# FNet and product-key experts in one kernel: scales summed by the matrix engine, second keys earlier, row sums spread over four blocks

## The chip, the cores and the metric

One core of a Trainium2 chip runs the whole program. The metric is its device time in microseconds (us). The engines are PE (TensorE, matmuls), DVE (VectorE), ACT (ScalarE), POOL (GpSimd) and SP (SyncE, which here only issues DMAs). Each engine works through its own list in order; an instruction waits for semaphores of other engines, and everything behind it on its engine waits with it. The programming layer places each instruction into its engine's list by a scheduler, so the order in a list isn't the order of the code.

## The reference

The input x has 2048 rows (tokens) of 512. The output is x plus two functions of its layer norm:

```python
def _A_ref(x, dft_seq_re, dft_seq_im, dft_hid_re, dft_hid_im):
    a = jnp.einsum("bsd,ed->bse", x, dft_hid_re)
    b = jnp.einsum("bsd,ed->bse", x, dft_hid_im)
    y = jnp.einsum("ts,bse->bte", dft_seq_re, a) - jnp.einsum("ts,bse->bte", dft_seq_im, b)
    return y

def _B_ref(x, w_q, k1, k2, u, v):                      # H=32 heads, dk=128, E=64, K=2, N=4096
    ...
    q = jnp.einsum("nd,dhc->nhc", xf, w_q)
    s1 = jnp.einsum("nhd,ed->nhe", q[..., :dk], k1)
    s2 = jnp.einsum("nhd,ed->nhe", q[..., dk:], k2)
    # the two best of s1, the two best of s2, of their four sums the two best: top_s, top_e
    ...
    g = _softmax(top_s, axis=-1)
    act = _gelu(jnp.einsum("nd,nhkd->nhk", xf, u[top_e]))
    out = jnp.einsum("nhk,nhk,nhkd->nd", g, act, v[top_e])
    return out.reshape(B, S, D)

xn = _layernorm(x, axis=-1)
return x + _A_ref(xn, ...) + _B_ref(xn, ...)
```

## The kernel before, in words

**Start (0 to some 80 us).** Rows of x come in four groups, in the order `G`, and are normalised (`ln`: statistics on DVE, the scaling on ACT and others). The Fourier transform uses its symmetries: `fold(k, g)` forms on DVE the sums (k = 0) or differences (k = 1) of a group's token pairs, folded once more over the columns, into the tile `q`; `main(k, g)` multiplies `q` by the cosine or sine table in fp32 on PE into four PSUM tiles `p` (L439). `evict(k)` brings `p` to SBUF on ACT (L491, L494). Token 512 (`x5`) and token 0 have no partner; `fold_row` folds token 512's row on POOL, and `sides` forms on DVE and POOL the rows that come from them. `stage(i)` splits a block of 128 normalised tokens into an fp16 high part (ACT, L509) and low part (DVE, L510), and SP issues two DMA transposes (L511) that lay the block out as weights `xt` for the score matmuls.

**Keys.** Instead of forming queries, the kernel multiplies w_q by the keys once: for each chunk j of four heads, `m_mul(j, t, ..)` runs 96 small matmuls (L135; L139 for chunk 0) of the four tiles t of w_q, and `m_parts` turns their sums into the operand `m`, as an fp16 high and low part (L219 on ACT, L220 on DVE). `m_prep(j, t, ..)` has to split w_q's tile first: high part on ACT (L149), the scaled tile on ACT (L151) or POOL (L153), low part on POOL (L154). So that fp16 holds the values, everything is scaled by powers of two: `w_sums` and `w_scale` get them for w_q and the keys, `absmax` and `uv_scale` for the experts' weights u and v. Both use `pow2`: an all-reduce across partitions on POOL (L109) and a few small DVE instructions (L110 to L113). `w_scale` also makes the index constants (`iota`, `io_lam`, `io_c`, `hoff`) on POOL.

**Routing (to some 430 us).** `part_b` runs over chunks j = 0 to 7 and over 16 blocks i of 128 tokens. A block is 12 score matmuls (L245, three products of high and low parts for four slices of 128), an ACT copy to one of four buffers `ss` (L837), and on DVE eight MAX8 (L841) and two FIND_INDEX8 (L845); `routing` then forms the pairs and softmax weights of the whole chunk. Eight blocks of chunk 0 run already in the start (`early`). Some columns of chunk 1's operand serve as buffers' first values: a copy to `EV` (L900), which the MAX8 of most of chunk 0's blocks have to follow. Other work is hung on blocks by hand: `m_stage` and `m_prep` for later chunks, `sums()` at block 10 of chunk 0 (26 small fp32 matmuls for rows 256 and 512 of the transform, L620 to L630), the hidden transforms `y_rows` (dictionary `HID`, L515 to L518 on PE), and the list `todo` (loads and maxima of u and v, `uv_scale` at place 14, later weights).

**Experts.** The rest (over 60% of the time) multiplies the tokens by all 4096 experts' u (L975), builds the weights' matrix from the routing (L1003 to L1013), and multiplies by v (L1058). A planner fills these phases; guards (`compare`, `fit`, `verdict`) watch that the scaled values fit fp16, and raise a flag that starts a plain recomputation.

PSUM has eight banks here: four for `pa` (scores, `p`), two for `pb`, two for `pc`; `m_mul` takes two of `pb` and two of `pc`.

Of the kernel before, what the change touches and what calls it, by code (L numbers as in the profile page):

```python
# [18 lines left out]
P = 128  # L19
# [5 lines left out]
NCH = 8  # L25
# [9 lines left out]
def tile_fnet_peer(ctx, tc, x, ca, cb, c5, wt, wf, wr, wq, kt, ut, vn, out):  # L35
# [47 lines left out]
    NW = 4 * (NCH - 1)  # L83
# [21 lines left out]
    def pow2(mx, pool, name, w=1, r=None, low=1e-30):  # L105

        m = pool.tile([P, 4, w], F32, tag=f"pow2_{w}", name=name, bufs=2 if w == 1 else 1)
        r = m[:, 0] if r is None else r
        nc.gpsimd.partition_all_reduce(r, mx, P, bass_isa.ReduceOp.absmax)  # L109
        nc.vector.tensor_scalar(m[:, 1], r, low, None, op0=ALU.max)  # L110
# [31 lines left out]
    def m_prep(j, t, pool, at):  # L142
# [7 lines left out]
        if j == 1 or t > 1:  # L150
            nc.scalar.activation(raw, raw, AF.Copy, scale=at)  # L151
        else:
            nc.gpsimd.tensor_scalar(raw, raw, sw, None, op0=ALU.mult)  # L153
        nc.gpsimd.tensor_tensor(l, raw, h, op=ALU.subtract)  # L154

    def m_stage(j, pool, stage):
# [5 lines left out]
        elif stage == 5 and (j, 0, "h") in MS:  # L162
            M[j] = MP[j % 2].tile([P, 2, KD, 512], F16, tag="m", name=f"m{j}"), inv1
            MS[j, "s"] = 2.0 ** -11
            m_fit(j - 1, M[j][0])
# [5 lines left out]
    def m_fit(j, junk):  # L171
        nc.scalar.activation(junk[:, 0], M[j][0][:, 0], AF.Abs, accum_out=fits[:, NW + 32 + j:NW + 33 + j])

# [15 lines left out]
    def w_sums():  # L189
# [4 lines left out]
        mx = MP[0].tile([P, 2], F32, tag="mx", name="mx")  # L194
# [7 lines left out]
    def w_scale(mx, low):  # L202

        with tc.tile_pool(name="iop", bufs=1, side="right") as iop:
            iof = iop.tile([P, P], F32, name="iof")
            p, q = pow2(mx, MP[0], "pw", 2, iof[:, 0:2], low)
            nc.gpsimd.iota(iof, pattern=[[1, P]], base=0, channel_multiplier=0,
                           allow_small_or_imprecise_dtypes=True)
            nc.gpsimd.tensor_copy(io_lam, iof)
            nc.gpsimd.tensor_scalar(io_c, iof[:, :NC], float(P), None, op0=ALU.mult)  # L210
            nc.gpsimd.tensor_scalar(hoff, iof[:, :HC], 64.0, None, op0=ALU.mult)
        nc.vector.tensor_scalar(wsc[:, 0:2], q, 2.0 ** 12, None, op0=ALU.mult)
        nc.vector.scalar_tensor_tensor(sm0, q[:, 0:1], 2.0 ** 13, q[:, 1:2], op0=ALU.mult, op1=ALU.mult)
        nc.vector.scalar_tensor_tensor(inv1, p[:, 0:1], 2.0 ** -15 / XS, p[:, 1:2], op0=ALU.mult, op1=ALU.mult)
# [79 lines left out]
    for t in Q[1]:  # L294
        nc.gpsimd.memset(t[:, :, 0:1], 0.0)
    A = {}
# [15 lines left out]
    SM = {}  # L312
# [5 lines left out]
    FT = {}  # L318
    zs = da.tile([P, 2], F32, name="zs")

    def ln(g, n):


        if n > 1:
# [1176 lines left out]
```

## Time and profile before

| what | value |
|---|---|
| median of the runs | 1158.45 us |
| lowest run | 1157.1 us |
| profiled execution | 1159.15 us |
| its span in the profile | 1157.3 us |
| PE busy | 1131.3 us, 98% |
| DVE busy | 930.0 us, 80% |
| ACT busy | 608.5 us, 53% |
| POOL busy | 256.3 us, 22% |

The span runs from the first to the last instruction in the trace, and the 1.85 us beside it lie around the program. In the rows of a timeline stand the start and the duration in us, engine, line, operation, output and inputs by the program's names, size, and the number of equal instructions drawn together; in brackets stands how long the engine was idle before, and which instruction ended that. In the rows of windows stand the stretch and then the busy time of PE, PE's weight load, DVE, ACT and POOL with their numbers of instructions, the granted clock of PE, the share of the DMA engines, and GB/s.

### The profile page before, as it was taken

How to read it: one execution, taken by the hardware profiler on the slowest of the kernel's cores; microseconds unless marked ns; L12 is line 12 of the kernel's file. 1: busy time of each engine (PE TensorE's matmuls, PEld its weight loads, DVE VectorE, ACT ScalarE, POOL GpSimd, SP SyncE). 2: the span in 40 equal slices, each digit the busy share in tenths (PEclk: the TensorE clock that was granted, in tenths of full speed). 3: DMA queues.
4: the chain of work that ended last, by engine and by line, in shares of the span. 5: the costliest groups of instructions: out<-in, count | busy, mean ns of one | idle time of the engine just before them, and what ended most of it. 6: DMA issues, size and time to landing. Idle time of an engine off the chain costs nothing.

```text
span 1157.3 us, 25208 instructions
## 1 busy us (share of the span) xinstructions
PE 1131.3 (98%) x9862; PEld 719.8 (62%) x9862; DVE 930.0 (80%) x2846; ACT 608.5 (53%) x1045; POOL 256.3 (22%) x226
## 2 busy tenths in 40 slices
PE   5999899999999999999999999999999999999997
PEld 4445455445445459778478479569569559658763
DVE  7979789799898998974994895897886886788670
ACT  7765487686786735354435435535535436433440
POOL 2371464865865411000000000010010000000000
PEclk9998899999999999999999999999999999999999
DMA  9992345243241204261743743654555555452423
GB/s 344 229 254 90 129 132 176 63 163 128 74 164 47 83 15 125 84 213 38 245 148 105 233 163 107 220 162 137 185 159 174 169 172 168 156 167 63 138 75 104
DMA packets 98335, 167.82 MB, mean 145 GB/s; under 512 B 32916, under 2 KB 48155, under 8 KB 98206
## 3 DMA queue, kind: packets, MB, share of 16 engines
q1 hardware_dynamic: 97904, 166.04, 44.5%
q8 instruction: 79, 1.29, 0.5%
q14 instruction: 50, 0.41, 0.1%
q10 hardware_dynamic: 302, 0.08, 0.0%
HBM read 142.69 MB, written 17.63 MB: 139 GB/s over the span
## 4 chain that ended last, share of the span: by engine, by line
PE 63%; DVE 21%; POOL 7%; issue 3%; ACT 3%; DMA 2%; SPq 0%; POOLq 0%; DVEq 0%; ACTq 0%
PE v L1058 28%; PE z L975 26%; DVE vals L841 5%; PE s L245 5%; DVE idx L845 4%; PE g L1013 4%; POOL w L153 2%; POOL w L154 2%; POOL u L722 1%; DVE z L782 1%; DVE L L1003 1%; DVE m L220 1%; DVE ft L406 1%; DVE z L783 1%; DVE u L510 1%
## 5 line engine op out<-in xcount | busy, mean ns | idle before, releaser
L975 PE MATMUL z<-xb,u 128*128 128x256 f16 (+1 forms) x3840 | 342.7, 251 | 0.2 <-ACT w L982 0.2
L975 PEld LDWEIGHTS <-u 128*128 128x128 f16 x3840 | 309.7, 98 | 26.7 <-issue 0.3
L245 PE MATMUL s<-m,xq 128*128 128x512 f16 x1344 | 301.4, 383 | 0.0
L1058 PE MATMUL v<-v,act 128*128 128x512 f16 x1056 | 233.2, 379 | 0.0
L245 PEld LDWEIGHTS <-xq 128*128 128x128 f16 x1344 | 131.0, 99 | 155.0 <-issue 7.0
L1003 DVE TENSOR_TENSOR L<-io_lam,cmp 128x2048 f16<-128x2048 f16 x128 | 156.0, 1219 | 62.2 <-PE g L1013 62.1
L1058 PEld LDWEIGHTS <-act 128*128 128x128 f16 x1056 | 101.3, 98 | 117.6
L1071 POOL TENSOR_TENSOR y<-y,xr 128x512 f32<-128x512 f32 x15 | 28.1, 1874 | 612.9 <-DMA y<-y_d 393.1
L841 DVE MAX8 vals<-ss 128x8 f32<-128x64 f32 x896 | 133.6, 216 | 2.7 <-ACT ss L837 2.5
L982 ACT ACTIVATE act<-z,scl 128x256 f32<-128x256 f32 (+1 forms) x152 | 72.7, 502 | 119.4 <-PE z L975 119.3
L837 ACT ACTIVATE ss<-s,wsc 128x512 f32<-128x512 f32 x120 | 80.7, 682 | 57.5 <-PE s L245 50.4
L1058 PE MATMUL v<-v,w 128*128 128x512 f16 x480 | 106.2, 379 | 0.0
L1134 ACT ACTIVATE cx<-cx 128x896 f32<-128x896 f32 x64 | 60.4, 945 | 68.5 <-DVE cx L1114 47.3
L845 DVE FIND_INDEX8 idx<-vals,ss 128x8 uint16<-128x256 f32 x224 | 93.8, 419 | 0.0
L1028 ACT ACTIVATE act<-w 128x1024 f16<-128x1024 f32 x36 | 48.3, 1358 | 62.6 <-DVE w L1021 62.1
L1058 PEld LDWEIGHTS <-w 128*128 128x128 f16 x480 | 46.0, 98 | 53.4
L154 POOL TENSOR_TENSOR w<-w,wh 128x1024 f16<-128x1024 f32 x28 | 70.7, 2530 | 19.0 <-ACT w L151 18.0
L1021 DVE SCALAR_TENSOR_TENSOR w<-act,scl,g 128x1024 f32<-128x1024 f32 x44 | 55.7, 1275 | 19.8 <-ACT act L982 19.8
L1108 DVE TENSOR_TENSOR cx<-cx 128x512 f32<-128x512 f32 (+2 forms) x84 | 48.5, 612 | 24.8 <-DMA cx<-in_cb_dram 18.3
L1013 PEld LDWEIGHTS <-L 128*128 128x128 f16 x2048 | 60.7, 96 | 11.7 <-DVE R L1011 1.3
L1011 DVE TENSOR_TENSOR R<-R,cmp 128x512 f16<-128x512 f16 x128 | 61.5, 480 | 1.5
L1013 PE MATMUL g<-R,L 128*128 128x32 f16 x2048 | 61.8, 176 | 0.7 <-DVE R L1011 0.6
(298 smaller groups left out, 1310.9 us busy)
## 6 DMA issues: line engine op xcount, KB each, us to landing
v<-v_d SPq DMA_DIRECT2D x67, 512.0 KB, 4.2
cx<-in_cb_dram SPq DMA_DIRECT2D x64, 448.0 KB, 4.2
w<-in_wq_dram SPq DMA_DIRECT2D x28, 512.0 KB, 5.5
fit<-in_wq_dram SPq DMA_DIRECT2D x28, 512.0 KB, 4.6
uv<-in_vn_dram SPq DMA_DIRECT2D x16, 512.0 KB, 3.8
uv<-in_ut_dram SPq DMA_DIRECT2D x16, 512.0 KB, 6.8
c<-in_ca_dram SPq DMA_DIRECT2D x8, 512.0 KB
y<-y_d SPq DMA_DIRECT2D x16, 256.0 KB, 2.6
```

The source lines that it names most:

```text
L154: nc.gpsimd.tensor_tensor(l, raw, h, op=ALU.subtract)
L245: nc.tensor.matmul(ps, xt[i][:, l, kd, :], m[:, r, kd, :], start=(n == 0), stop=(n == 3 * KD - 1))
L837: nc.scalar.activation(s, ps, AF.Copy, scale=inv)
L841: nc.vector.max(vals[:, i, w, :, h], s[:, g, :])
L845: nc.vector.max_index(idx[:, i, w].rearrange("p k h -> p (k h)"), vals[:, i, w, 0:2].rearrange("p k h -> p (k h)"), s[:, w * HC:g + 1, :]. ...
L975: nc.tensor.matmul(ps if n == 1 else ps.rearrange("p (b n) -> p b n", b=2), ug[:, l, c % 2, kd, :], xb2[:, k0, r, kd, :] if n == 1 else xb ...
L982: nc.scalar.activation(ACT[bb][:, cg * m:cg * m + m, :], pv[:, i], AF.Gelu_apprx_tanh, scale=zsc)
L1003: nc.vector.tensor_tensor(L.rearrange("p t (l two) -> p t l two", two=2), io_lam.rearrange("p (l two) -> p l two", two=2).unsqueeze(1).to_ ...
L1011: nc.vector.tensor_tensor(Rv, Rv, bc(2, NC), op=ALU.mult)
L1013: nc.tensor.matmul(p[:, hf, t * NC:(t + 1) * NC], L[:, t, :], R[:, t, :], start=True, stop=True)
L1058: nc.tensor.matmul(pv, w16[:, c, :, l], v_sb[g][:, r, cc, :], start=(n + cc == 0 and k == 0), stop=(n == 15 and cc == 1 and k == 2))
L1134: later.append(lambda: nc.scalar.activation(tf[:, P:], tf[:, P:], AF.Abs, accum_out=chk[:, n:n + 1]))
```

## The change

- **Scales.** `pow2` takes a PSUM tile `total` in which PE has summed the partitions' values by a matmul with a tile of ones, 128 x 128. The sum over 128 partitions stands in for the maximum, so the constants move by 2^7. `w_scale` and `uv_scale` use it; the recomputation keeps the all-reduce. The matmul for w_q follows `w_sums`; that for u and v lies in a `pc` bank.
- **Constants and token 512.** `iota` and what is made from it stand at the start, on POOL, apart from token 512's row, which is normalised by ACT. Two products of `sides` go from POOL to ACT, two sums from POOL to DVE. The statistics' scratch lies elsewhere, and a copy of four columns in the second group's fold goes from ACT to DVE.
- **Chunk 1's keys.** The high parts of all four tiles come right after the second difference; the low parts are formed by DVE in one instruction (`m_low`), and `m_mul(1, ..)` stands in front of `main(1, 3)`. The copy to `EV` serves all 16 blocks at once. The last four `stage` stand behind `sides`.
- **Row sums.** `sums(part)` runs in four parts at blocks 9 to 12. `y_rows`, `absmax`, `uv_scale` and one `m_fit` move to later places.

```diff
+    ones = cst.tile([P, P], F32, name="ones")
+    nc.gpsimd.memset(ones, 1.0)
...
-    def pow2(mx, pool, name, w=1, r=None, low=1e-30):
+    def pow2(mx, pool, name, w=1, total=None, low=1e-13):
         m = pool.tile([P, 4, w], F32, tag=f"pow2_{w}", name=name, bufs=2 if w == 1 else 1)
-        r = m[:, 0] if r is None else r
-        nc.gpsimd.partition_all_reduce(r, mx, P, bass_isa.ReduceOp.absmax)
-        nc.vector.tensor_scalar(m[:, 1], r, low, None, op0=ALU.max)
+        if total is None:
+            nc.gpsimd.partition_all_reduce(m[:, 0], mx, P, bass_isa.ReduceOp.absmax)
+            nc.vector.tensor_scalar(m[:, 1], m[:, 0], 1e-30, None, op0=ALU.max)
+        else:
+            if mx is not None:
+                nc.tensor.matmul(total[:, 0:w], ones, mx, start=True, stop=True)
+            nc.vector.tensor_scalar(m[:, 1], total[:, 0:w], low, None, op0=ALU.max)
...
         nc.scalar.activation(h, raw, AF.Copy, scale=at)
-        if j == 1 or t > 1:
+        if j == 1:
+            return
+        if t > 1:
             nc.scalar.activation(raw, raw, AF.Copy, scale=at)
         else:
             nc.gpsimd.tensor_scalar(raw, raw, sw, None, op0=ALU.mult)
         nc.gpsimd.tensor_tensor(l, raw, h, op=ALU.subtract)
+
+    def m_low(j, t, at):
+        raw = MS[j, t].rearrange("p h k -> p (h k)")
+        nc.vector.scalar_tensor_tensor(MS[j, t, "l"].rearrange("p h k -> p (h k)"), raw, at,
+                                       MS[j, t, "h"].rearrange("p h k -> p (h k)"), op0=ALU.mult, op1=ALU.subtract)
...
-        if g == 0:
-            for q in range(2):
-                nc.gpsimd.tensor_scalar(x5[:, q], x5[:, q], mvs[0:1, 0, q + 2, 0:1], rstd[0:1, 0, q + 2:q + 3],
-                                        op0=ALU.subtract, op1=ALU.mult)
...
         if n == 0:
-            wmx = w_sums()
+            wtot = pa("wsum")
+            nc.tensor.matmul(wtot[:, 0:2], ones, w_sums(), start=True, stop=True)
         if n == 1:
-            nc.scalar.activation(zs[:, 0:1], rstd[:, g, 0:1], AF.Copy, scale=0.0)
+            nc.scalar.activation(zs[:, 0:1], xn(g, 3)[:, 0:1], AF.Copy, scale=0.0)
             for q in range(4):
                 stage(4 * G[0] + q)
+            for q in range(2):
+                nc.scalar.activation(x5[:, q], x5[:, q], AF.Identity, bias=negm[0:1, 0, q + 2:q + 3],
+                                     scale=rstd[0:1, 0, q + 2:q + 3])
...
+        if g == 3:
+            for t in range(4):
+                m_low(1, t, s5c[:, 0, 0:1])
+            for t in range(4):
+                m_mul(1, t, range(KD))
         main(1, g)
-        if g > 1:
-            for t in range(2 * g - 4, 2 * g - 2):
+        if g == 1:
+            for t in range(4):
                 m_prep(1, t, whp, s5c[:, 0, 0:1])
-    for g in (2, 3):
-        for q in range(4):
-            stage(4 * g + q)
+    for q in range(4):
+        stage(8 + q)
     sides()
+    for q in range(4):
+        stage(12 + q)
     evict(1)
...
-            p, q = pow2(mx, wqp, f"uvp{safe}", 2)
+            p, q = pow2(mx, wqp, f"uvp{safe}", 2, None if safe else pc("uvs"))
...
-        HID = {11: 8, 12: 0, 13: 1, 14: 2, 15: 3, 27: 4, 29: 5, 30: 6, 32: 7}
+        HID = {13: 8, 14: 0, 15: 1, 16: 2, 17: 3, 27: 4, 29: 5, 30: 6, 32: 7}
...
-            for which, n in ((0, 8), (1, 13)):
+            for which, n in ((0, 10), (1, 15)):
...
-            todo[8].append(lambda at: am_load(1, 0))
-            todo[14].append(lambda at: uv_scale())
+            todo[10].append(lambda at: am_load(1, 0))
+            todo[18].append(lambda at: uv_scale())
+            todo[20].append(lambda at: m_fit(0, uf[15].bitcast(F16).rearrange("p (k n) -> p k n", k=KD)))
...
-                for a, b in ((0, 4), (6, NT)):
+                for a, b in ((0, NT),):
...
-                if j == 0 and i == 10 and not safe:
-                    sums()
+                if j == 0 and 9 <= i < 13 and not safe:
+                    sums(i - 9)
```

Where the scheduler puts this is seen in the engines' lists. The first place is DVE's list at the second group's fold: `ft`, `ff`, `fo` are its steps, `q_0` its result for PE, `u` from `x` the low parts of blocks, `m` the key parts of chunk 0. Before:

```order
L510 TENSOR_TENSOR u_123<-x_140,u_123 128x512
L510 TENSOR_TENSOR u_124<-x_141,u_124 128x512
L510 TENSOR_TENSOR u_130<-x_141,u_130 128x512
L385 TENSOR_TENSOR ff_0_303<-ft_0_340 128x4x127
L220 SCALAR_TENSOR_TENSOR m_241<-m_0_197,wsc,m_241 128x512
L394 TENSOR_TENSOR fo_0_341<-ff_0_303 128x2x128
L395 TENSOR_TENSOR fo_0_341<-ff_0_303 128x2x128
L220 SCALAR_TENSOR_TENSOR m_241<-m_1_200,wsc,m_241 128x512
L409 TENSOR_TENSOR q_0_142<-fo_0_341 128x257
```

And now, from the fold's first addition on:

```order
L390 TENSOR_TENSOR ff_0_337<-ft_0_336 128x4x127
L513 TENSOR_TENSOR u_125<-x_142,u_125 128x512
L399 TENSOR_TENSOR fo_0_338<-ff_0_337 128x2x128
L400 TENSOR_TENSOR fo_0_338<-ff_0_337 128x2x128
L513 TENSOR_TENSOR u_125<-x_142,u_125 128x512
L412 TENSOR_TENSOR q_0_144<-fo_0_338 128x257
L413 TENSOR_TENSOR q_0_144<-fo_0_338 128x257
L513 TENSOR_TENSOR u_126<-x_143,u_126 128x512
L513 TENSOR_TENSOR u_132<-x_143,u_132 128x512
L228 SCALAR_TENSOR_TENSOR m_249<-m_0_204,wsc,m_249 128x512
```

Two of the four low parts and all of the key parts now follow `q_0`.

The second place is SP's list near 47 us, where block 1 to 7's transposes are issued (`xb`, `xq` from `u`), beside the load of u for its maxima (L685, now L705) and copies of `xt` to memory (L908, now L930). Before:

```order
L511 DMA_TRANSPOSE xb_96<-u_131 128x8x128
L511 DMA_TRANSPOSE xq_100<-u_131 128x8x128
L511 DMA_TRANSPOSE xq_100<-u_123 128x8x128
L685 DMA u_135<-in_ut_dram 128x2x512
L908 DMA xt_d<-xb_96 128x1024 x2
L511 DMA_TRANSPOSE xq_103<-u_123 128x8x128
```

And now:

```order
L514 DMA_TRANSPOSE xb_98<-u_133 128x8x128
L514 DMA_TRANSPOSE xq_102<-u_133 128x8x128
L705 DMA u_137<-in_ut_dram 128x2x512
L514 DMA_TRANSPOSE xq_102<-u_125 128x8x128
L930 DMA xt_d<-xb_98 128x1024 x2
L930 DMA xt_d<-xq_102 128x1024 x2
L514 DMA_TRANSPOSE xq_105<-u_125 128x8x128
```

The load of u stands between the two transposes of `xq_102`.

The third place is POOL's list at chunk 2's weights (`w` and `wh`), where the all-reduce (ISA rows) stood. `c` is the routing of chunk 0. Before:

```order
L154 TENSOR_TENSOR w_119<-w_119,wh_0_1120 128x1024
L109 ISA
L109 ISA uvpFalse<-asums 128x2
L153 ISA
L153 TENSOR_SCALAR w_119<-w_119,wsc 128x1024
L154 TENSOR_TENSOR w_119<-w_119,wh_2_1290 128x1024
L154 TENSOR_TENSOR w_119<-w_119,wh_1_1217 128x1024
L770 TENSOR_TENSOR c_0_1320<-u_127 128x64
L771 TENSOR_TENSOR c_0_1321<-u_127 128x64
L772 TENSOR_TENSOR c_0_1322<-u_127 128x64
L154 TENSOR_TENSOR w_119<-w_119,wh_3_1378 128x1024
```

And now:

```order
L163 TENSOR_TENSOR w_121<-w_121,wh_0_1085 128x1024
L162 TENSOR_SCALAR w_121<-w_121,wsc 128x1024
L163 TENSOR_TENSOR w_121<-w_121,wh_1_1170 128x1024
L791 TENSOR_TENSOR c_0_1305<-u_129 128x64
L792 TENSOR_TENSOR c_0_1306<-u_129 128x64
L793 TENSOR_TENSOR c_0_1307<-u_129 128x64
L163 TENSOR_TENSOR w_121<-w_121,wh_2_1260 128x1024
L796 TENSOR_TENSOR c_0_1305<-c_0_1306,c_0_1305 128x64
L163 TENSOR_TENSOR w_121<-w_121,wh_3_1374 128x1024
```

No reduction stands between the four tiles, and `c` comes ahead of the third.

More of the change, by code (lines that the diff above doesn't have):

```diff
@@ L200, in w_sums, with w_scale @@
         return mx
[L202 to L214, printed above, removed]
+    def w_scale(total, low):
+        p, q = pow2(None, MP[0], "pw", 2, total, low)
+        nc.vector.tensor_scalar(wsc[:, 0:2], q, 2.0 ** 19, None, op0=ALU.mult)
+        nc.vector.scalar_tensor_tensor(sm0, q[:, 0:1], 2.0 ** 27, q[:, 1:2], op0=ALU.mult, op1=ALU.mult)
+        nc.vector.scalar_tensor_tensor(inv1, p[:, 0:1], 2.0 ** -29 / XS, p[:, 1:2], op0=ALU.mult, op1=ALU.mult)
     def m_parts(j, pm):
@@ L577, in tile_fnet_peer @@
                 stage(q)
[L578 to L583 removed]
+        if n:
+            main(0, g)
         if n == 1:
```

123 lines of the change are left out of this document (65 added, 58 removed).

## The prediction

> **What bounds the kernel now.** I read the engine totals and the chain first, then TensorE's (PE's) waits, then the timeline around each of them, and the granted clock in short windows.
>
> ```profile
> span 1157.3 us, 25208 instructions
> PE 1131.3 (98%) x9862; PEld 719.8 (62%) x9862; DVE 930.0 (80%) x2846; ACT 608.5 (53%) x1045; POOL 256.3 (22%) x226
> PE 63%; DVE 21%; POOL 7%; issue 3%; ACT 3%; DMA 2%; SPq 0%; POOLq 0%; DVEq 0%; ACTq 0%
> ...
> PE m L139 <- DMA wq<-in_wq_dram: 9.2, 1, 9.2
> PE m L135 <- POOL w L154: 5.1, 2, 4.8
> PE p L439 <- DVE q L409: 3.8, 1, 3.8
> PE p L439 <- ACT u L491: 0.8, 1, 0.8
> ...
> 26.00:32.00 6.00, 3.75 (x5) 1.68 (x6) 6.00 (x13) 4.54 (x10) 5.92 (x10) 0.50 1.31 168
> 92.00:96.00 4.00, 4.00 (x11) 1.42 (x10) 4.00 (x28) 0.00 (x0) 0.00 (x0) 0.50 0.12 45
> 128.00:134.00 6.00, 3.79 (x29) 2.14 (x30) 2.97 (x7) 0.09 (x1) 5.39 (x7) 0.50 0.54 189
> 136.00:240.00 104.00, 104.00 (x698) 52.99 (x694) 92.41 (x487) 76.01 (x131) 60.61 (x59) 1.00 0.41 137
> ```
>
> PE is busy 98% of the span. Its waits up to 240 us are the four rows, 18.9 us, and the last window shows PE filled without a gap at full clock from 136 us on. So what PE gains or loses before 136 us moves the end by as much, and what is saved on the other engines counts only where PE waits for it. Besides the waits there are three stretches in which the granted clock is 0.50 (in the windows the column after POOL's busy time), and each makes matmuls take twice as long. The change touches the waits of 4.8 and 3.8 us, the 0.8, and the second and third slow stretch. The first 9.2 us are the wait for the first weights and stay.
>
> **Part 1, scales from sums by PE.** Before, two all-reduces on GpSimd (POOL) find the largest of the row sums across partitions. The second, for u and v, sits in the middle of the preparation of chunk 2's weights:
>
> ```profile
> 106.84 2.14 POOL L154 TENSOR_TENSOR w<-w,wh 128x1024 f16<-128x1024 f32 x1
> 115.50 0.37 POOL L109 PARTITION_ALL_REDUCE uvpFalse<-asums  x1 [6.52 <-ACT u L523]
> 123.12 2.85 POOL L153 TENSOR_SCALAR w<-w,wsc 128x1024 f32<-128x1024 f32 x1 [7.25 <-ACT ss L837]
> 125.96 4.19 POOL L154 TENSOR_TENSOR w<-w,wh 128x1024 f16<-128x1024 f32 x2
> 130.21 0.24 PE L135 MATMUL m<-sums,w 128*128 128x64 f16 x1 [4.77 <-POOL w L154]
> 131.38 4.30 PE L245 MATMUL s<-m,xq 128*128 128x512 f16 x12
> 136.22 5.34 PE L245 MATMUL s<-m,xq 128*128 128x512 f16 x24
> 131.03 2.13 DVE L773 TENSOR_TENSOR pm<-c,c 128x64 f32<-128x64 f32 x1 [6.71 <-POOL c L772]
> 104.61 2.75 PE L245 MATMUL s<-m,xq 128*128 128x512 f16 x12
> ```
>
> The reduction takes 0.37 us, but POOL does nothing from 108.98 to 123.12 except it: 14.1 us. The low halves of the weights (L154) then end at 130.15, and PE's next key matmul has waited 4.77 us for them. The pause brings the third slow stretch: twelve score matmuls take 4.30 us where twelve take 2.75 (1.55 lost), and the small ones around them double too; I put the stretch at 2.2 us. DVE stands behind the same queue: its routing (L773) waits 6.71 us for POOL. Without the reduction the first two pairs of POOL (2.85 + 2.14 = 5.0 us each) can end near 111 and 116, as ScalarE (ACT) delivers, and the third and fourth low half near 121 and 125, some 5 us ahead of PE. Gain 4.77 + 2.2 = 7.0. What hides the new work: each total is one PE matmul with ones, 128x2 in fp32; 16 matmuls of that form take 1.84 us (the L620 row below), 0.12 each. With the switch between them I take 0.3 us for both.
>
> [...]
>
> **Part 1's new wait.** The total for u and v lies in one of two PSUM buffers (`pc`) that the key matmuls `m2` use as well. VectorE (DVE) has to read it before PE can run `m2_1`, and on DVE the read stands behind the MAX8/FIND_INDEX8 of chunk 1's first blocks. By the count under part 3 it comes near 126.5, and PE, at its pace since 111.57, wants the buffer near 126.3: 0.3 us; bounds 0 and 4 (two blocks of DVE), beyond which a slow stretch would come on top.
>
> **Part 2, token 512's row and iota.** The row's two instructions leave POOL:
>
> ```profile
> 21.49 6.16 POOL L373 TENSOR_SCALAR u<-u,mvs,rstd 1x512 f32<-1x512 f32 x2 [9.36 <-DVE wsc L213]
> 22.03 0.66 DVE L510 TENSOR_TENSOR u<-x,u 128x512 f16<-128x512 f32 x1
> 27.79 0.41 DVE L409 TENSOR_TENSOR q<-fo 128x257 f32<-128x257 f32 x1
> 28.25 5.61 PE L439 MATMUL p<-c,q 128*128 128x512 f32 x8 [3.80 <-DVE q L409]
> 33.70 10.52 PE L245 MATMUL s<-m,xq 128*128 128x512 f16 x48
> ```
>
> They are off PE's path; on ACT they cost 2 x 0.7 us (an L509 below) in a place with idle time. What matters is that DVE's order around the second group's fold changes: `q` now comes after two, not four, of the 0.66-us splits (L510), and ahead of the key parts L220, two of which stood before it (0.62 each, from the 2.48 for four below). 2 x 0.66 + 2 x 0.62 = 2.6, so `q` is ready near 25.5 and the 3.80 us wait falls to about 1.1; scores start near 30.8.
>
> This gain meets another queue. ACT issues in order; between the evictions of `p` stands a split of x that waits for a DMA transpose:
>
> ```profile
> 50.31 0.54 SPq L685 DMA_DIRECT2D u<-in_ut_dram  x1
> 52.34 0.72 ACT L509 ACTIVATE u<-xq,zs 128x512 f16<-128x512 f32 x1 [1.47 <-DMA xq<-u]
> 53.02 0.59 ACT L491 ACTIVATE u<-p 128x512 f32<-128x512 f32 x1
> 52.51 0.38 PE L245 MATMUL s<-m,xb 128*128 128x512 f16 x1
> 53.66 2.84 PE L439 MATMUL p<-c,q 128*128 128x512 f32 x6 [0.77 <-ACT u L491]
> 24.00:26.00 2.00, 0.45 (x5) 0.32 (x3) 2.00 (x6) 1.68 (x3) 1.99 (x2) 0.82 1.03 406
> ```
>
> Now the 512-KB load of u is queued between the two transposes, no longer behind them. At the 406 GB/s that the last row shows, 512 KB are 1.3 us. The transpose then lands near 53.5 (52.3), the eviction that PE needs ends near 54.7, and PE resumes near 54.9 instead of 53.66: 1.2 later, although it has run dry 3 us earlier, near 49.6. Bounds: -3 (the transposes pass the load, and the whole gain is kept) to +3. The new pause is 5.3 us, longer than the 4.77 that ended in a slow stretch above, so I add one, 2.2 us (bounds 0.5 and 3.4). The stall of 0.3 at the first L154 is gone. Sum of the start: +1.2 + 2.2 - 0.3 = **+3.1**.
>
> [...] No row here shows this pause yet.
>
> **Part 3, second keys in front of the last difference.** The key matmuls of chunk 1 (96) move ahead of `main(1,3)` on PE; their number stays. Their low halves go from ACT (L151) and POOL (L154) to DVE in one instruction each.
>
> ```profile
> 71.93 0.59 DVE L841 MAX8 u<-u 128x8 f32<-128x64 f32 x4
> 72.85 0.60 DVE L841 MAX8 u<-u 128x8 f32<-128x64 f32 x4
> 84.08 2.48 DVE L220 SCALAR_TENSOR_TENSOR m<-m,m 128x512 f16<-128x512 f32 x4 [8.40 <-ACT m L219]
> L1021 DVE SCALAR_TENSOR_TENSOR w<-act,scl,g 128x1024 f32<-128x1024 f32 x44 | 55.7, 1275 | 19.8 <-ACT act L982 19.8
> 110.51 0.27 DVE L527 TENSOR_TENSOR u<-u,hy 128x127 f32<-128x127 f32 x1
> 111.57 5.34 PE L245 MATMUL s<-m,xb 128*128 128x512 f16 x24
> ```
>
> Four of the form of L1021 are 5.1 us of DVE, placed among the last difference's fold, ahead of PE, which reaches these matmuls near 75. What hides them is the 8.40 us in which DVE stood idle for ACT before 84.08: the sides that follow move 5 us into it. But two blocks of MAX8/FIND_INDEX8 that filled the time just before that idle (71.93 to 75.68) now come after the key parts, since all 16 blocks take their constants from one copy. The parts end near 87, as before (ACT no longer runs its 2-us check L172 ahead of them, but PE comes 3 us later); from there 16 blocks are left and not 14. Half a block lies between the rows at 71.93 and 72.85, 0.92, so a block is 1.84 us and DVE is 3.7 us further behind. PE uses 2.6 us a block (5.34 for two), so DVE wins 0.75 a block. Four score buffers and four PSUM buffers lie between. DVE frees the score buffer of tile 8 after nine blocks, 87.1 + 9 x 1.84 = 103.7; PE needs the PSUM behind it at (1,0), near where that began before, 111.57. The margin is some 7 us, so I cost this at 0 on the scores. The read of the total stands after 19 blocks and the five hidden rows' 20 adds of some 0.2 (0.27 each, overlapping): 87.1 + 35.0 + 4 = 126.1, with the wait's remainder the 126.5 above.
>
> **Part 4, row sums amid blocks 9 to 12.**
>
> ```profile
> 87.88 1.84 PE L620 MATMUL b<-w,u 128*128 128x2 f32 x16
> 90.22 1.01 PE L630 MATMUL b<-one,u 128*128 128x1 f32 x4
> 91.10 6.94 PE L245 MATMUL s<-m,xq 128*128 128x512 f16 x18
> ```
>
> The same 26 small matmuls in four pieces of at most 1 us. In one piece they are 3.2 us, and the clock falls right behind them: 18 scores take 6.94 us where 1.5 times 2.6 = 3.9 would do, 3.0 lost, with the small ones in it 3.4. Split, twelve full matmuls stand between any two pieces, and I take the whole 3.4 (bounds 0 and 3.4). The hidden rows, absmax and scales come one to four blocks later; PE does the same work.
>
> **Sum.** +3.1 (start) - 3.4 (row sums) - 7.0 (POOL) + 0.3 (matmuls with ones) + 0.3 (the read of the total) = -6.7. The profiled execution took 1159.15 us, 1.85 above its span, and its median is 1158.45; I take the sum from the median: **1151.7**.
>
> **Rivals.**
>
> *The start's gain is kept.* DVE's earlier `q` counts for 2.9 us and neither the load between the transposes nor a slow stretch takes it back. For it: the load is issued in 0.54 us, and no row shows a transpose kept back by one. Against: ACT's 1.47 us wait for the transpose is already the last one. -2.9 - 3.4 - 7.0 + 0.6 = -12.7: 1145.7.
>
> *The start loses more.* The transpose comes one length later (1.3) and the slow stretch is as dear as the second one (3.4, not 2.2): -6.7 + 2.5 = -4.2: 1154.2.
>
> *The other side: the total's PSUM buffer waits for DVE.* Place: PE at `m2_1`, in block (1,2). In DVE's new order the routing instruction that waited 6.71 us for POOL (the row at 131.03) stands eight instructions ahead of the read of the total, and the wait would now hold PE. If it stays, PE stands 6.7 + 0.3 us, which brings a slow stretch: -7.0 + 7.0 + 2.2 = +2.2: 1160.7. It is slower than before from a wait of 4.8 us on. For it: POOL waits for ACT, and ACT for DVE's score buffers, in a ring. Against: POOL's `c` now stands ahead of the third low half, with no reduction in front.
>
> *The change does not do what it says on POOL.* ACT's high halves for chunk 2 stand behind copies of scores that wait for DVE; if they come 14 us late, POOL's low halves are as late as they were and the 7.0 stay away: 1158.7.
>
> **Chances.** Forecast 0.45, gain kept 0.18, start loses more 0.15, total waits 0.15, POOL as late as before 0.07. From 1143.5 (the kept gain with no slow stretch at all at the start, some 2 us more) to 1161 holds about 0.85. All cases lie within 23 us, which is 2% and about what a measurement of this kernel can tell from no change: within 0.96, faster by more 0.02, slower by more 0.02, the rests for a mechanism that none of these rows shows.
>
> **What would show it.** In the changed profile: no all-reduce row near 115; PE's waits without the row of 4.8 us; the granted clock at 1.00 between 88 and 136; `p` restarting near 25.5; a wait of PE on ACT's eviction near 50 of some 5 us with a clock of 0.5 behind it; block (1,6), which is the x24 group that started at 136.22, at about 129.5. It is wrong if PE waits for DVE between 118 and 135, if the pause near 50 is missing, or if anything later than 140 us moves apart from the shift.

## The result, and the profile after

The changed kernel takes 1158.40 us (median of 12 runs, 1157.05 to 1160.18), the kernel before 1158.30 us (12 runs, 1156.6 to 1159.17 but for one of 3012.29). The ratio is 1.0004, 95% interval [0.9995, 1.0013]: no change. Forecast were 1151.7 us, within 1143.5 to 1161. Behind the start the change gained 8.3 us of the 9.8 that were forecast there, and the start lost 7.5 of them.

The two profiled executions lie on different sides of their medians (before 1159.15, after 1157.52): the traces differ by 1.6 us where the medians differ by 0.1. The first page and PE's waits up to 260 us, after the change (without the first one, 9.3 us for the first weights):

```profile
span 1155.7 us, 25202 instructions
PE 1128.8 (98%) x9866; PEld 719.0 (62%) x9866; DVE 935.7 (81%) x2853; ACT 606.8 (53%) x1045; POOL 223.9 (19%) x216
...
PE p L442 <- ACT u L494: 5.1, 1, 5.1
PE p L442 <- DVE q L412: 4.1, 2, 3.9
PE m L142 <- DVE uvpFalse L117: 1.2, 1, 1.2
PE hy L518 <- DVE u L530: 0.5, 1, 0.5
```

PE's wait for POOL (5.1 us, of them 4.8 in one piece) is gone. In its place stands the wait for ACT's eviction of `p` from PSUM, 0.8 us before and 5.1 now. Two small waits for DVE are new, 1.2 us for the total of u and v (`uvp`) and 0.5 at a hidden row (`hy`). The windows that answer to those before (stretch, busy times of PE, its weight load, DVE, ACT, POOL, then the granted clock):

```profile
26.00:32.00 6.00, 3.13 (x4) 1.51 (x5) 6.00 (x10) 5.90 (x11) 4.15 (x6) 0.50 0.92 151
54.00:60.00 6.00, 0.90 (x1) 0.50 (x2) 6.00 (x14) 2.22 (x6) 0.00 (x0) 0.72 1.05 316
92.00:96.00 4.00, 4.00 (x25) 2.32 (x24) 4.00 (x29) 2.02 (x4) 0.00 (x0) 1.00 0.97 356
128.00:134.00 6.00, 4.79 (x54) 2.64 (x53) 5.40 (x23) 3.63 (x5) 4.35 (x7) 1.00 0.08 25
136.00:240.00 104.00, 104.00 (x686) 52.81 (x685) 92.72 (x490) 76.47 (x130) 59.09 (x54) 1.00 0.48 158
```

The slow stretches near 93 and near 131 are gone, as forecast; the one near 28 stays, and a new one follows the pause near 56. PE's timeline at the places where the steps of the sum can be read; the last row is that of block 8 in the kernel before:

```profile
28.87 5.59 PE L442 MATMUL p<-c,q 128*128 128x512 f32 x8 [3.87 <-DVE q L412]
53.59 0.38 PE L253 MATMUL s<-m,xb 128*128 128x512 f16 x1
59.10 4.97 PE L442 MATMUL p<-c,q 128*128 128x512 f32 x6 [5.13 <-ACT u L494]
87.59 5.34 PE L253 MATMUL s<-m,xq 128*128 128x512 f16 x24
113.70 4.26 PE L253 MATMUL s<-m,xb 128*128 128x512 f16 x19
132.38 0.22 PE L142 MATMUL m<-sums,wh 128*128 128x64 f16 x2 [1.22 <-DVE uvpFalse L117]
135.37 5.34 PE L253 MATMUL s<-m,xq 128*128 128x512 f16 x24
...
80.11 7.93 PE L245 MATMUL s<-m,xq 128*128 128x512 f16 x36
```

Block 8 of chunk 0 (87.59) began at 80.11 before, chunk 1 (113.70) at 111.57, block (1,6), which is block 6 of chunk 1, (135.37) at 136.22. So the start lost 7.5 us, the stretch from there to chunk 1 won 5.3, the stretch from chunk 1 to (1,6) won 3.0. Two hidden rows of 0.89 us (100.24 to 101.13 before) moved from the second stretch into the third. Without this move the second stretch, that of the row sums, won 3.6 us, and the third, that of the total and POOL, 4.8.

Behind the 5.13 us stand these rows of SP, ACT, DVE and POOL:

```profile
51.31 1.23 SPq L514 DMA_TRANSPOSE xq<-u  x1
52.64 0.53 SPq L705 DMA_DIRECT2D u<-in_ut_dram  x1
53.26 1.24 SPq L514 DMA_TRANSPOSE xq<-u  x1
51.62 0.58 ACT L494 ACTIVATE u<-p 128x512 f32<-128x512 f32 x1
57.78 0.72 ACT L512 ACTIVATE u<-xq,zs 128x512 f16<-128x512 f32 x1 [5.58 <-DMA xq<-u]
58.46 0.59 ACT L494 ACTIVATE u<-p 128x512 f32<-128x512 f32 x1
21.96 1.74 DVE L390 TENSOR_TENSOR ff<-ft 128x508 f32<-128x508 f32 x1
26.29 1.75 DVE L513 TENSOR_TENSOR u<-x,u 128x512 f16<-128x512 f32 x1
39.44 0.16 DVE L367 SCALAR_TENSOR_TENSOR negm<-mvs,rstd 128x4 f32<-128x4 f32 x1
43.17 1.23 DVE L409 TENSOR_TENSOR ft<-xq,xq 128x1024 f32<-128x1024 f32 x1 [3.57 <-ACT xq L379]
21.89 1.26 POOL L418 TENSOR_TENSOR r<-u 1x512 f32<-1x512 f32 x1 [8.49 <-ACT u L576]
```

Two rows of the kernel before that they are compared with:

```profile
27.84 1.81 POOL L415 TENSOR_TENSOR r<-u 1x512 f32<-1x512 f32 x1
35.33 0.16 DVE L358 SCALAR_TENSOR_TENSOR negm<-mvs,rstd 128x4 f32<-128x4 f32 x1
```

The first block, read from the bottom: ACT has token 512's row ready sooner, so POOL's fold of it starts at 21.89 (27.84 before), and DVE's fold and splits, which run beside it, take up to 1.1 us more each (0.68 and 0.66 before for the same lines). The last group's statistics end at 39.44 instead of 35.33, DVE idles 3.57 us for ACT's normalisation, its next fold step comes at 43.17 (38.49 before), the transposes are issued 3.8 and some 4.4 us later, and ACT's split (L512), which waits 5.58 us for a transpose to land, holds the eviction behind it. That is the reading; the runs below say which of its links count.

### The profile page after: what moved, and what is told of

Read it like the earlier page. It is cut to its first block, busy times and chain, and to the rows that moved or that the text cites. A ratio compares the mean times of both kernels' runs of the same rounds, so it can differ in the third digit from the quotient of the medians.

```text
span 1155.7 us, 25202 instructions
## 1 busy us (share of the span) xinstructions
PE 1128.8 (98%) x9866; PEld 719.0 (62%) x9866; DVE 935.7 (81%) x2853; ACT 606.8 (53%) x1045; POOL 223.9 (19%) x216
## 4 chain that ended last, share of the span: by engine, by line
PE 89%; DVE 8%; ACT 1%; DMA 1%; issue 0%; DVEq 0%; ACTq 0%
PE z L997 29%; PE v L1080 28%; PE s L253 25%; PE g L1035 4%; PE m L142 2%; DVE u L862 1%; PE p L442 1%; DVE u L866 1%; DVE u L513 1%; DVE ft L409 1%; DVE sums L358 0%; DVE m L228 0%; DVE L L1025 0%; DMA xq<-u 0%; DVE ff L390 0%; DMA x<-in_x_dram 0%
## 5 line engine op out<-in xcount | busy, mean ns | idle before, releaser
L253 PE MATMUL s<-m,xq 128*128 128x512 f16 x1344 | 297.6, 379 | 0.0
L1004 ACT ACTIVATE w<-z,scl 128x256 f32<-128x256 f32 (+1 forms) x72 | 35.4, 492 | 49.3 <-PE z L997 49.3
```

The lines of the kernel that those rows point to most:

```text
L253: nc.tensor.matmul(ps, xt[i][:, l, kd, :], m[:, r, kd, :], start=(n == 0), stop=(n == 3 * KD - 1))
L1004: nc.scalar.activation(ACT[bb][:, cg * m:cg * m + m, :], pv[:, i], AF.Gelu_apprx_tanh, scale=zsc)
```

## The experiments

All ratios are against the kernel before, run on the same chip; in the brackets behind them stands the 95% interval. The expectations call "theory 1" that POOL's earlier fold beside DVE costs the start its time; "theory A" is that the split's place in ACT's list does.

**Fold of token 512's row later.** In the changed kernel POOL's fold waits for the last group's constants:

```diff
         if n == 3:
             nc.scalar.activation(zs[:, 1:2], rstd[:, G[3], 0:1], AF.Copy, scale=0.0)
+            nc.scalar.activation(x5[:, :, 0:1], x5[:, :, 0:1], AF.Identity, bias=zs[0:1, 1:2])
             fold_row(0)
```

> The changed kernel, but POOL's fold of token 512's row waits for the last group's statistics (one ACT instruction of two elements on the row), so that it runs near 40 us and not from 21.9 to 30.3. DVE's list is the same, row for row. Theory 1 (POOL's two-input instructions beside DVE's hold DVE up: L390 took 1.74 us for 0.68, L513 1.75 for 0.66, about 4 us in all from 22 to 31): p restarts near 25.7 instead of 28.87, tile 8 of chunk 0 starts about 4 us earlier than 87.59, the time is near 1154.5. Theory 2 (the row's two normalisations on ACT delay the splits and so all that follows) and theory 3 (DVE's new order is itself slower): nothing moves, 1158.4.

Measured: 1158.39 us, ratio 1.0005 [0.9995, 1.0014]. DVE, ACT and PE of that run:

```profile
22.26 0.69 DVE L390 TENSOR_TENSOR ff<-ft 128x508 f32<-128x508 f32 x1
35.71 0.16 DVE L367 SCALAR_TENSOR_TENSOR negm<-mvs,rstd 128x4 f32<-128x4 f32 x1
40.59 1.76 DVE L513 TENSOR_TENSOR u<-x,u 128x512 f16<-128x512 f32 x1
25.65 3.70 PE L442 MATMUL p<-c,q 128*128 128x512 f32 x8
47.84 5.20 PE L442 MATMUL p<-c,q 128*128 128x512 f32 x8 [4.17 <-DVE q L412]
59.40 5.39 PE L442 MATMUL p<-c,q 128*128 128x512 f32 x6 [4.55 <-ACT u L494]
```

With POOL away from it L390 takes 0.69 us, the statistics end 3.7 us earlier, and `p` restarts at 25.65: the prediction's 25.5. The local claim of theory 1 holds. But POOL's fold now runs from 39.7 to 50 beside the next folds (40.59), PE waits 4.17 us there, and the wait for the eviction is nearly as long as it was. As it was expected, with some 4 us won, theory 1 falls. The run doesn't clear the collision of the late transposes, though: it moves the collision, and ACT's split waits for its transpose until 58.07, as late as in the changed kernel (57.78). What it shows of the first collision is its price on DVE: the fold step that came at 43.17 comes at 39.44, so 3.7 of its 4.7 us of lateness were POOL's, and the other 1.0 stays with DVE's new order.

In the changed kernel L390 started at 21.96, behind POOL's 1.26 us from 21.89 on, of which 1.19 were left, and took 1.74 us, with POOL away 0.69, so 1.05 less. What the two engines share there, and whether it matters that both instructions have two inputs, no run shows.

**Load of u later.** The 512-KB load follows the transposes:

```diff
+            nc.gpsimd.tensor_copy(uf[15][:, 0:1], MS[1, 3, "h"][:, 0, 0:1])
             am_load(0, 0)
```

> The changed kernel with the first load of u held back (by one element written from a later tile) until the high parts of chunk 1's weights exist, so that SP issues it after the transposes near 60 us. If the load between the transposes is what delays the transpose, the split that ACT waits for comes 1.1 to 1.5 us earlier than 57.78 and tile 8 as much, 1157. If the transpose is late only because its inputs are late: 57.78 stays within 0.3, 1158.4.

Measured: 1158.22 us, ratio 1.0001 [0.9991, 1.0010].

```profile
57.71 5.29 PE L442 MATMUL p<-c,q 128*128 128x512 f32 x8 [4.71 <-ACT u L494]
86.51 5.34 PE L253 MATMUL s<-m,xq 128*128 128x512 f16 x24
```

PE resumes 1.4 us earlier than in the changed kernel and block 8 comes 1.1 earlier. So the load between the transposes costs about what the prediction gave it (1.2), and it is the small part of the 5.4 us by which PE resumes later than in the kernel before (59.10 against 53.66). The time as a whole does not show this 1 us.

**Token 512's row back to POOL**, in the changed kernel:

```diff
+        if g == 0:
+            for q in range(2):
+                nc.gpsimd.tensor_scalar(x5[:, q], x5[:, q], mvs[0:1, 0, q + 2, 0:1], rstd[0:1, 0, q + 2:q + 3],
+                                        op0=ALU.subtract, op1=ALU.mult)
...
-            for q in range(2):
-                nc.scalar.activation(x5[:, q], x5[:, q], AF.Identity, bias=negm[0:1, 0, q + 2:q + 3],
-                                     scale=rstd[0:1, 0, q + 2:q + 3])
```

> The changed kernel with the normalisation of token 512's row back on POOL, as before the change (its start is not held back by an all-reduce now). Theory 1: POOL's two-input fold still runs beside DVE's second fold, near 20 to 29 us, so p still restarts after 27.5 and the time is within 1.5 us of 1158.4. Theory 2: ACT's 1.6 us are gone, the eviction after 50 us comes 1.6 to 4 us earlier, 1154.5 to 1157.

Measured: 1151.89 us, ratio 0.9942 [0.9925, 0.9958], faster than either theory allowed (theory 1: within 1.5 us of 1158.4; theory 2: 1154.5 to 1157). It looks as if the row's place on ACT had cost the time, and the rows say otherwise:

```profile
39.43 0.16 DVE L367 SCALAR_TENSOR_TENSOR negm<-mvs,rstd 128x4 f32<-128x4 f32 x1
53.61 0.60 ACT L498 ACTIVATE u<-p 128x512 f32<-128x512 f32 x1 [0.26 <-PE p L446]
57.76 0.72 ACT L516 ACTIVATE u<-xq,zs 128x512 f16<-128x512 f32 x1 [1.75 <-DMA xq<-u]
81.47 5.34 PE L253 MATMUL s<-m,xq 128*128 128x512 f16 x24
```

DVE's statistics end as late as in the changed kernel (39.43 and 39.44), and the split waits for its transpose until the same 57.7. What differs is ACT's list: here the scheduler put the split behind the evictions (53.61), so PE does not wait for it, and block 8 comes 6.1 us earlier than in the changed kernel. POOL's fold lies beside DVE's here too (from 21.55 on): the collision alone does not cost the time. Nor does POOL's early fold need the move of the row to ACT: with the first reduction gone, POOL begins with the row at 17.22 (21.49 before).

**Token 512's row to ACT, in the kernel before** (the reverse edit).

> The kernel before with one part of the change alone: token 512's row is normalised by ACT, all else as it was (both all-reduces, row sums in one piece). POOL's fold of the row then moves from 27.8 to 37 us up to about 21.5 to 31. Theory 1: DVE's instructions from 21.5 on take up to 1 us longer each, p restarts at 30 to 32 instead of 28.25, and the time is 3 to 5 us above before, 1161.5 to 1163. Theory 2: ACT's 1.6 us show in the splits at most, 1158.5 to 1160.

Measured: 1157.08 us, ratio 0.9989 [0.998, 0.9999]: no loss. `q` came later (PE waits 4.4 us for it, 3.8 before), but here too the scheduler placed two evictions ahead of the split, and PE waited 0.2 us for ACT instead of 0.8. Theory 1's loss of 3 us or more did not appear. The run says less about it than was meant: with the first reduction still there POOL's fold began at 24.50 and not at 21.5.

**Only the place in ACT's list.** The changed kernel; the splits of the last four blocks take as zero bias the column of `zs` that is made after the evictions, so the scheduler has to put them behind. Two of the four stood there already. Of the other two, one stood between the evictions and one some 5 us ahead of them:

```diff
-        nc.scalar.activation(t[:, 0], src, AF.Identity, bias=zs[:, int(n > 3):int(n > 3) + 1])
+        nc.scalar.activation(t[:, 0], src, AF.Identity,
+                             bias=zs[:, 2:3] if i >= 12 else zs[:, int(n > 3):int(n > 3) + 1])
```

> The changed kernel with one instruction of ACT's list moved: the split of block 12, which waits for a transpose, takes its zero bias from a tile that is made after the evictions of p, so it stands behind them (DVE's and POOL's lists are as in the changed kernel). Theory A (what costs the time is this one place in ACT's list, and the late transpose matters only through it): PE's wait of 5.13 us near 59 and the slow stretch behind it are gone, tile 8 starts near 80.5 to 81.5 instead of 87.59, 1151.5 to 1152.5. Theory B (the transposes come late for PE in any case, and the kernel with token 512's row back on POOL was faster since ACT has 1.6 us less to do): PE waits elsewhere for most of it, 1155.5 to 1158.4.

Measured: 1150.97 us (1150.68 to 1151.7), ratio 0.9941 [0.9925, 0.9958], 0.5 us below what theory A expected.

```profile
51.78 1.18 ACT L494 ACTIVATE u<-p 128x512 f32<-128x512 f32 x2
60.90 0.70 ACT L512 ACTIVATE u<-xq,zs 128x512 f16<-128x512 f32 x1
80.22 5.34 PE L253 MATMUL s<-m,xq 128*128 128x512 f16 x24
```

The eviction wait and its slow stretch are gone, both evictions run in one go at 51.78, and block 8 comes at 80.22 instead of 87.59. SP issues the transposes as late as in the changed kernel (0.16 us apart), and DVE's and POOL's rows up to there are the same, so their lateness costs nothing by itself. The other split that moved gives ACT 0.7 us of idle time near 47.6, but the evictions begin no earlier for it (51.78 and 51.62). So the place of one 0.7-us instruction, between the evictions, is worth 7.4 us here: theory A holds.

**The same with POOL's fold held until some 31 us**, between DVE's two folds:

```diff
+            z5 = da.tile([1, 1], F32, name="z5")
+            nc.scalar.activation(z5, negm[0:1, G[2], 0:1], AF.Copy, scale=0.0)
+            nc.scalar.activation(x5[:, :, 0:1], x5[:, :, 0:1], AF.Identity, bias=z5)
             fold_row(0)
```

> As the run with the moved split, and POOL's fold of token 512's row also waits (one ACT instruction of two elements) until ACT is done with the key parts near 31 us, so that DVE's second fold has no two-input instruction of POOL beside it. Theory A and POOL's two-input instructions as the cause of DVE's lateness: p restarts near 25.7 instead of 28.87, the third group's statistics end near 36 instead of 39.4, tile 8 starts 2 to 4 us earlier than with the moved split alone, 1148.5 to 1150.5. If the two-input instructions only hit other folds: no earlier than with the moved split alone, 1151.5 to 1152.5.

Measured: 1152.67 us, ratio 0.9948 [0.9931, 0.9965]: 1.7 us above the last run, with intervals that overlap; in the traces block 8 comes 1.8 us later (82.06). `p` restarts at 25.62, but then PE waits:

```profile
47.80 6.36 PE L442 MATMUL p<-c,q 128*128 128x512 f32 x8 [4.25 <-DVE q L412]
```

Three places for POOL's fold (22, 31 and 40 us) give three places of collision and none a better end; 31 was tried with the split moved, 40 only without.

**Row sums alone**, in the kernel before: `sums(part)` at blocks 9 to 12 and the hidden rows two blocks later, as in the change.

> The kernel before with the row sums alone in four parts at blocks 9 to 12 and the hidden rows two places later; the all-reduces stay. The prediction's own step gives 3.4 us off, 1154.9. Rival: PE arrives 3.4 us earlier at the key matmuls of chunk 2 and waits so much longer there, since POOL's low halves (4.77 us late) keep their time: the slow stretch near 93 is gone from the trace, the wait near 130 grows to about 8, 1158 to 1158.5.

Measured: 1156.73 us, ratio 0.9988 [0.9978, 0.9997]. The slow stretch near 93 is gone, but PE now waits 3.2 us for DVE's part of the hidden rows (0.9 at 110, 0.2 and 2.1 at 120 to 123): of 3.4 us, 1.4 arrive. The wait for POOL near 130 did not grow, as the rival had it, but fell from 4.8 to 2.6 us.

**The total of u and v by PE alone**, in the kernel before (the central lines of the edit):

```diff
+            nc.tensor.matmul(total[:, 0:w], ones, mx, start=True, stop=True)
+            r = total[:, 0:w]
...
-            p, q = pow2(mx, wqp, f"uvp{safe}", 2)
+            p, q = pow2(mx, wqp, f"uvp{safe}", 2, total=None if safe else pc("uvs"))
```

> The kernel before with the total for u and v alone summed by PE (a matmul with ones into a pc bank, at the old place 14; the first all-reduce stays). The prediction's step: the wait of 4.77 us and the slow stretch of 2.2 us at 128 go, 7.0 off, 1151.4. Rival: a wait for the pc bank or for ACT takes 1 to 3 us of it, 1152.5 to 1154.5.

Measured: 1152.99 us, ratio 0.9954 [0.9937, 0.997]. The wait for POOL near 130 is gone; PE at block 8, behind the row sums, and at block (1,6):

```profile
81.72 7.93 PE L252 MATMUL s<-m,xq 128*128 128x512 f16 x36
92.61 5.40 PE L252 MATMUL s<-m,xq 128*128 128x512 f16 x18
130.29 5.34 PE L252 MATMUL s<-m,xq 128*128 128x512 f16 x24
```

Block 8 came 1.6 us later than in the kernel before and block (1,6) 5.9 earlier: 7.5 us won between the two. 1.5 of them belong to the 18 scores behind the row sums, which took 5.40 us and not 6.94, though the edit doesn't touch them; 6.0 are left for the total (forecast: 7.0, less 0.3 for the matmuls). The time lies where the rival had it, but the wait that the rival names isn't there; what is missing was lost ahead of block 8.

What holds POOL around the reduction stays open. The row of the kernel before names ACT's copy (L837) for the 7.25 us behind it; that copy ended at 122.82, 0.3 us ahead of POOL's next instruction (123.12). In POOL's list an ISA instruction stands on either side of the reduction; whether the copy, these or the reduction itself take the time, no run separates.

**Both of these together**, in the kernel before.

> The kernel before with two parts of the change: the row sums in four pieces (hidden rows two blocks later) and the total of the u/v maxima by PE's matmuls with ones. Start, token 512's row, POOL's and ACT's lists there and the second keys are as before. Alone, the first gave -1.6 us and the second -5.1 us. Theory 1 (both steps of the prediction are right in size where nothing else moves; the row sums' 3.4 us were masked alone by the wait for POOL near 130): about -8.5 us, 1149.5 to 1151, ratio 0.993, no slow stretch near 93, no wait for POOL of 2 us near 130. Rival (the hidden rows that come two blocks later take the gain of the row sums back, whatever POOL does): -5 to -6.5 us, 1152 to 1153.5, ratio 0.995, with a wait of PE of over 1.5 us near 130.

Measured: 1154.1 us, ratio 0.9969 [0.9957, 0.9982]; neither 8.5 nor even 5.1 us better. PE:

```profile
54.45 4.54 PE L446 MATMUL p<-c,q 128*128 128x512 f32 x6 [2.12 <-ACT u L498]
82.07 5.34 PE L252 MATMUL s<-m,xq 128*128 128x512 f16 x24
110.71 0.35 PE L114 MATMUL uvs<-asums,ones 128*128 128x2 f32 x2 [1.93 <-DVE u L534]
130.17 5.34 PE L252 MATMUL s<-m,xq 128*128 128x512 f16 x24
```

Block 8 is 2.0 us late, and from there to (1,6) 8.0 are won: the two steps (3.4 and 6.0 or a little more) add up between these blocks, less a new wait of 1.9 us for the last hidden row. The steps have the sizes that theory 1 gave them, and the hidden rows take part of it back, as the rival said, by a wait near 110 and not near 130. In the change itself that wait isn't there; it moves `uv_scale` from place 14 to 18.

**Both, and the splits behind the evictions.** The edit is that of the order run, in the kernel before.

> The kernel before with the row sums in four pieces and the total of the u/v maxima by PE (as in the run that gave 1154.1 us), and the splits of blocks 12 to 15 made behind the evictions of p, as in the run that gave 1150.97 us. In the run without the last edit, PE waited 2.12 us for the eviction, six matmuls after it took 4.54 us where six took 2.84, and block 8 came 2.0 us later than in the kernel before. Theory (the split's place in ACT's list costs wherever the transposes come late, not only in the changed kernel): no wait of PE on the evictions, six matmuls in 2.8 us, block 8 near 78.5 to 79.5, the time 3 to 4 us shorter than 1154.1: 1150 to 1151.3, ratio 0.993 to 0.994. Rival (the late transposes themselves hold PE, through the scores that need them): PE waits later by as much, for xt or for a split, and the time stays within 1 us of 1154.1.

Measured: 1153.88 us, ratio 0.9956 [0.994, 0.9972]; 0.2 us better, which is no difference, and not 3 to 4. The wait for the eviction is gone and block 8 comes 1.6 us earlier, at 80.44, but 0.9 us of waiting for POOL's low halves is new there, and the wait near 110 grew:

```profile
110.25 0.35 PE L114 MATMUL uvs<-asums,ones 128*128 128x2 f32 x2 [3.10 <-DVE u L534]
```

So the theory holds for the wait and the slow stretch behind it and fails for the sum. Here other queues stand right behind this one.

**The kernel before with the order edit alone.**

> The kernel before with one edit: the splits of blocks 12 to 15 behind the evictions of p. In the kernel before PE waits 0.77 us for that eviction, and no slow stretch follows. Theory (the place costs what PE waits there, plus a slow stretch only where the pause is long): -0.5 to -1.5 us, 1156.8 to 1157.8, no wait on the evictions. Rival (ACT's list there costs more than PE's wait shows, because later key parts come sooner): -3 us or more. A second rival (the time moves by nothing, since the waits of 4.8 us for POOL near 130 take the gain back): -0.5 to 0.

Measured: 1158.08 us, ratio 0.9995 [0.9986, 1.0003], by the second rival. PE no longer waits for the eviction (0.8 us before), and waits 6.7 us for POOL's low halves (5.1 before), 2.7 of them at the keys of chunk 1, where it was 0.4:

```profile
PE m L135 <- POOL w L154: 6.7, 3, 4.0
...
78.48 0.20 PE L135 MATMUL m<-sums,w 128*128 128x64 f16 x1 [1.49 <-POOL w L154]
80.56 0.20 PE L135 MATMUL m<-sums,w 128*128 128x64 f16 x1 [1.21 <-POOL w L154]
```

The same edit is worth 7.4 us in the changed kernel, where PE had waited 5.1 us for the eviction with a slow stretch behind, and DVE makes chunk 1's low halves; in the kernel before there were 0.8 us to be had, and POOL took them.

**A better version.** The order edit, and the total of u and v in a bank of `pa` and not of `pc`, so that `m2_1` need not wait until DVE has read it:

```diff
-            p, q = pow2(mx, wqp, f"uvp{safe}", 2, None if safe else pc("uvs"))
+            p, q = pow2(mx, wqp, f"uvp{safe}", 2, None if safe else pa("uvs"))
```

> The changed kernel with the two zero-bias splits behind the evictions of p (as in the run that gave 1150.97 us), and the total of the u/v maxima in PSUM of the scores' pool, no longer in that of the routing, so the routing's matmuls wait for no read of the total. Theory (the wait of 1.2 us at m2_1, and 0.5 us at hy behind it, come from the total's place alone): about -1.5 us against that run, 1149.3 to 1150, block (1,6) near 126.5. Rival (PE had slack to the score buffers there, or the score buffer that the total takes makes the scores wait): 1150.5 to 1152, with a wait of PE on DVE or POOL of 1 us or more between 115 and 135.

Measured: 1149.46 us (1148.72 to 1150.78), ratio 0.9925 [0.9911, 0.9938]: 0.75% faster than the kernel before, and 1.5 us below the run with the order edit alone. The two were run on different chips and their ranges touch; in the traces block (1,6) comes 1.3 us earlier (126.69 against 127.99). Of PE's waits up to 260 us, the one for `uvp` (1.2 us) is gone. The 0.5 us at the hidden row, which the expectation put down to the total too, stay. Besides the 9.7 us for the first weights one wait of more than 0.5 us is left:

```profile
PE p L442 <- DVE q L412: 3.2, 1, 3.2
```

## Why the prediction was wrong

Term by term, as the blocks of the two traces give it:

| step | forecast | measured |
|---|---|---|
| start, to block 8 | +3.1 | +7.5 |
| row sums | -3.4 | -3.6 |
| POOL without the reduction, with the matmuls and the new wait | -6.4 | -4.8 |
| sum | -6.7 | -0.85 at block (1,6); 0.1 by the medians |

- **The step that failed is in part 2**: "`q` is ready near 25.5", and from it "the transpose then lands near 53.5". They were out by 3.4 and 4.3 us: `p` restarted at 28.87, the split ran at 57.78. The prediction took POOL's two instructions for token 512 to be "off PE's path" and costed only what they take on ACT. It did not ask what POOL does once it is free of them, and of the first reduction: its fold comes 6 us earlier, beside DVE's. Each of the two moves the fold forward alone (to 24.50 with the row on ACT, to 21.55 with the reduction gone). In the run with the late fold the 25.5 come true: with that taken away `p` restarts at 25.65.
- **The link from there to PE was seen and read too softly.** The split between two evictions was quoted, with a 1.47-us wait, and its place taken as given. What counted was that an eviction stands behind one of the late transposes: with the transposes as late as ever, taking the split from between the evictions brings block 8 from 87.59 to 80.22, and it was 80.11 before. So the +3.1 of the start were no price of the load and the pause as such, but of this one place.
- **The sizes behind the pause came out right, one of them by luck**: a pause of 5.13 us (5.3 forecast), a slow stretch of 2.1 us (six matmuls in 4.97 against 2.84; 2.2 forecast), the load 1.4 us (1.2). PE ran dry near 54.0 and resumed at 59.10, 4.4 and 4.2 us later than written, and that is the miss of the start; the pause between has its length because both ends slipped alike. The forecast's own working is loose there too: `q` comes 2.6 us earlier, the scores 2.9 and the end of PE's work 3.3, without a term for the difference. With 2.6 throughout the pause would have been 4.6 us.
- **The total's new wait** was put at 0.3 us within 0 to 4; it was 1.2, with another 0.5 at the hidden row ahead of it. That is 1.4 us more than forecast, most of the 1.6 that the step lacks, and a wait of PE for DVE between 118 and 135 was one of the forecast's signs of being wrong. With the total in another bank the 1.2 are gone. Of the 0.3 us for the matmuls with ones, the total of u and v took 0.14 of PE's time between two groups of scores (123.99 to 124.13); the switch that the forecast adds to them is its author's estimate, and no row shows it apart.
- **Right**: no reduction in the way, no slow stretch between 88 and 136, row sums. From 136 to 240 us PE stays full. The trace ends 1.6 us earlier than before, 0.75 more than block (1,6) gained, which is less than the 3.1 us by which the runs of the changed kernel differ. The rival on the other side (routing holds the total 6.7 us) did not come. "The start loses more" named the place, and had it at 2.5 us where 4.4 were lost. The measured time lies near that of "POOL as late as before" (1158.7) by chance: the wait for POOL near 130 is gone.

What stays open: which order of folds would keep POOL's fold clear of DVE altogether (three places were tried, none is free), and so what the start would cost with the transposes early and the split in its place. That POOL's fold makes the transposes late rests on the rows and on the 3.7 us of the late fold; no run has them early in the changed kernel.

## What to carry to other kernels

When work leaves an engine, ask what that engine does next and beside whom; here POOL, off the path, started its fold 6 us earlier, DVE's addition beside it took 1.74 us and not 0.69, and `p` restarted at 28.87 and not at 25.65. In an engine's list look for an instruction that waits for a DMA and has a PSUM eviction behind it: here it cost 0.8 us while the DMA was early, and 5.1 us with a slow clock on top (0.50 from 58 to 62) when work upstream had made it some 4 us later. And a wait taken away doesn't always give its length: in the kernel with the split row sums and the total by PE, 2.1 us of wait and a slow stretch were removed and the time stayed, since PE waited elsewhere.

## What the runs showed that was not expected

- **A pause's length alone does not decide on the slow clock.** At the same place, pauses of 0.77 and 1.39 us (before, and with the total by PE) left six matmuls at 2.84 us; with 2.12 us (both parts together) the clock was 0.74 from 54 to 56 and 0.50 from 56 to 58, and they took 4.54. But near 110, amid fp16 scores, a pause of 3.10 us left the clock at 1.00 and eleven scores at 2.54 (both parts and the order edit). What decides, no run shows.
- **Small shifts change which DVE instructions are hit.** In the kernel before with the total by PE, where DVE's and POOL's instructions from 20 to 39 us come in the order of before, one addition `ft` took 2.20 us beside POOL and 1.18 before, one `q` 1.50 and 0.41, and block 8 came 1.6 us later. So the start differed here by 1.6 us from kernel to kernel without any part of the edit touching it; how far it does from one execution to the next, single traces don't show.
